# Attention, a Fourier mix and an MLP on one core: a second fold of the Fourier sums, narrower matmuls, layer norm sums by transposes, and a new order

## The chip, the core and the metric

The kernel runs on one core of a Trainium2 chip. A core has TensorE (PE in the profile, with its weight loads shown apart as PEld), VectorE (DVE), ScalarE (ACT), GpSimd (POOL) and SyncE (SP), which here only issues transfers. TensorE multiplies a stationary operand (up to 128 rows by 128 columns, loaded first) with a moving one (128 rows by up to 512 columns) and adds into PSUM, which has eight banks of 512 floats for each of 128 partitions. The metric is the device time of one execution in microseconds (us), the median of the runs.

## The reference, cut to what matters

```python
# q, k, v: (8, 8, 576, 64); s: (8, 8, 576)
scores = q @ k.transpose(0, 1, 3, 2) / 8
cum = np.cumsum(np.maximum(s, 0), -1)
bias = -(cum[..., :, None] - cum[..., None, :])
scores = np.where(causal, -1e9, scores + np.minimum(bias, 0))
attn = np.exp(scores - scores.max(-1, keepdims=True))
x = attn / (attn.sum(-1, keepdims=True) + 1e-9) @ v      # -> (8, 576, 512)
mixed = np.real(np.fft.fft(np.fft.fft(x, axis=1), axis=2))
u = x + mixed
un = (u - mean(u)) / np.sqrt(var(u) + 1e-6)               # over the 512 features
out = u + np.maximum(un @ w_ch1, 0) @ w_ch2               # 512 -> 2048 -> 512
```

## The kernel before

**Attention** runs over 32 pairs of heads (8 batches, 4 pairs each). For a pair `high` and `low` split q and k into two rounded parts, so that one-pass matmuls (float32r) give enough digits; the bias stands as extra rows of the same operands (`KQ`). `maxes` multiplies query chunks of 128 with all keys that they may see (`pm`, line 873) and DVE takes the largest with a causal mask added (`tri`, `trih`; lines 875 and 877). The maxima go by a PE transpose (`pmt`) and a transfer into another row of `KQ`. `scores` multiplies again, the key chunk now stationary (`ps`, lines 930 and 931), ACT writes exp into `P`, POOL clears the triangle. Head 0 is stored reversed and head 1 rotated by 64 positions, so that the corners of 64 keys of both heads share one product (line 941, `Px`). Products with fewer than 256 moving columns are padded to 256. `av` multiplies `va` (V | ones | V, 192 wide, a slice of 128 stationary) with `P` in float32, which takes several passes (`pavA`, `pavB`, lines 966 and 970); one output row is the sum of the weights. `recip` sends the sums through memory (`rd`, `rb`), `finish` scales and lays the result into `xa` and `xs`, in the order of features `_perm`.

**Fourier.** `folds` adds and subtracts features d and 512 - d (`xa` and `xs`) and positions t and 576 - t; `fourier` then multiplies over features with cosine and sine tables (`pzc`, line 677, and `pzs`, line 669: two halves of 128 features by three parts, 256 or 258 columns), over positions (`pyc`, `pys`, lines 691 and 700), and adds the result into `xa` and `xs`, which go to memory as `uD`. Seven batches are mixed in during attention, the eighth at the seam and beside the first MLP pieces.

**MLP.** The 4608 tokens are nine tiles of 512. `ln_tile` loads a tile u, forms mean and variance with a matrix of ones on PE (`spread_sum`, lines 486 and 487; four matmuls of 512 columns a tile) and splits the centred tile into `uch` and `ucl`. `mlp_tile` runs 16 steps f: twelve matmuls into `h` (line 557), ACT `zh`, DVE `zl` (line 562), and twelve matmuls of the step before into `acc` (lines 569 to 571). The end of a tile multiplies by r (line 588), adds u and stores.

**What sets the order.** Streams are written interleaved (`weave`), and `order` then arranges every engine's instructions up to the first whole MLP tile by a list schedule: estimated costs (`cost`), `HOLD`, `SLACK` and a table of rank offsets (`SHIFT`, `SEED`). Each engine works through its queue in that order. PSUM tiles come from two rings, `bank` (3 slots) and `m` (5 slots, attention only), taken in turn.

Of the kernel before, what the change touches and what calls it, by code (L numbers as in the profile page):

```python
# [60 lines left out]
SHIFT = {
    (PE, "acc"): (0, 0, 0, 0, 0, 0, 5866), (PE, "h"): (0, 0, 0, 0, 0, 0, -296), (PE, "mu"): (0, 2583, 0, 0, 0, 0, 341),
    (PE, "p"): (0, 0, 0, 0, -168, 0, -9), (PE, "pavA"): (-335, 0, -14, -4, 0, 52, 0), (PE, "pavB"): (6022, 42, 43, 43, 46, 5789, 0),
    (PE, "pm"): (18, 0, 0, 0, -1, 0, 0), (PE, "pmt"): (193, -48, 3, -2167, -254, 0, 0), (PE, "ps"): (-1361, 2, 0, 0, 3, 0, 0),
    (PE, "pyc"): (0, 0, 0, 54, 58, -602, -3), (PE, "pys"): (0, 0, 0, 6, 2, -61, 1), (PE, "pzc"): (0, 0, 0, -3, 0, -23, -315),
    (PE, "pzs"): (0, 0, -801, -2493, 0, 6667, 418), (PE, "var"): (0, 0, 0, 0, 0, 170, 5872),
    (DVE, "Aw"): (-240, 0, 0, 0, -2067, -16, 0), (DVE, "De"): (0, 0, 0, 0, -4837, 1161, 0), (DVE, "Df"): (0, -935, 0, 0, -12, 653, 0),
    (DVE, "Do"): (0, -201, 0, 0, -30, 0, 0), (DVE, "KQ"): (-267, 0, 0, 0, 0, 0, 0), (DVE, "M"): (-191, -2461, -792, -1216, -5948, 0, 0),
    (DVE, "Px"): (-45, 0, 0, 0, 0, 0, 0), (DVE, "cw"): (-16, 0, 0, 0, 0, 0, 0), (DVE, "e"): (0, 161, 0, 0, 0, 589, 0),
    (DVE, "eh"): (0, 209, 0, 0, 0, 0, 0), (DVE, "eps"): (-18, 0, 0, 0, 0, 0, 0), (DVE, "k"): (0, 95, 63, 117, 135, 0, 0),  # L70
    (DVE, "ones"): (303, 0, 0, 0, 0, 0, 0), (DVE, "part"): (0, 0, 0, 0, 0, 0, -298), (DVE, "r"): (0, 0, 0, 0, 0, -322, 839),
    (DVE, "rows"): (0, 0, 0, 0, -2506, 0, 65), (DVE, "sums"): (0, 52, -54, -2195, -1068, -3432, 0), (DVE, "t"): (0, -81, 0, 0, 0, 181, 8917),
    (DVE, "tl"): (0, -356, 0, 0, 0, 2, 32), (DVE, "trash"): (-131, -10028, -9581, -9808, -6968, 0, 0), (DVE, "u"): (0, 81, 0, 0, 0, 0, 33),
    (DVE, "ucl"): (0, 110, 0, 0, 0, 0, 3631), (DVE, "wbias"): (-109, 0, 0, 0, 0, 0, 0), (DVE, "we"): (-22, -71, -17, -34, 0, 0, 1348),
    (DVE, "wl"): (0, 0, 0, 0, 0, -73, -15), (DVE, "wm"): (423, -31, 50, 75, 35, 0, 1852), (DVE, "xr"): (0, 0, 0, 0, 0, -643, 0),
    (DVE, "ym"): (0, 0, 0, 0, -21, -149, -74), (DVE, "yp"): (0, 0, 0, 0, -1431, 74, -17), (DVE, "z"): (0, 0, 0, -2349, 0, 0, -42),
    (DVE, "zc"): (0, 0, -8299, -5757, 0, 0, 9), (DVE, "zl"): (0, 0, 0, 0, 0, 0, -1170), (DVE, "zs"): (0, 0, -13, 0, 0, -46, -154),
    (ACT, "De"): (0, 0, 0, 0, -41, 0, 0), (ACT, "Do"): (0, -598, 0, 0, 639, -30, 0), (ACT, "KQ"): (548, 1481, 197, 242, 2, 0, 0),
    (ACT, "P"): (0, 2, -444, 21, -4202, 0, 0), (ACT, "Px"): (-433, -5720, -5478, -101, -7966, 0, 0), (ACT, "cumhl"): (253, 0, 0, 0, 0, 0, 0),
    (ACT, "cw"): (823, 0, 0, 0, 0, 0, 0), (ACT, "eh"): (0, 26, 0, 0, 0, 34, 0), (ACT, "k"): (159, 0, 0, 0, 0, 0, 0),  # L80
    (ACT, "mt"): (-32, 112, -256, -58, 54, 0, 0), (ACT, "mu"): (0, 0, 0, 0, 0, 0, -11), (ACT, "part"): (0, 0, 0, 0, 0, 0, 478),
    (ACT, "q"): (62, 0, 0, 0, 0, 0, 0), (ACT, "r"): (0, 0, 0, 0, 0, 485, 153), (ACT, "stage"): (1691, 19, 357, -375, -951, 48, 0),
    (ACT, "sumrow"): (21, 138, -457, 0, 15, -36, 0), (ACT, "th"): (0, -275, 0, 0, 0, 404, 148), (ACT, "u"): (0, -55, 0, 0, 0, 0, 184),
    (ACT, "uch"): (0, 803, 0, 0, 0, 0, -199), (ACT, "we"): (-483, 2962, -459, 1931, 3, 0, 322), (ACT, "wh"): (0, 0, 0, 0, 0, 562, -21),
    (ACT, "yc"): (0, 0, 0, 136, -131, 570, -23), (ACT, "zc"): (0, 0, 4397, 597, 0, -732, -39), (ACT, "zh"): (0, 0, 0, 0, 0, 0, -162),
    (ACT, "zs"): (0, 0, -5, 920, 0, -191, -81),
    (POOL, "Bw"): (0, 0, 0, 0, -5280, 29, 0), (POOL, "KQ"): (248, 0, 0, 0, 0, 0, 0), (POOL, "P"): (428, -114, -255, 1127, -89, 0, 0),
    (POOL, "Px"): (-43, 419, -22, -276, 0, 0, 0), (POOL, "cor"): (0, 0, 0, 0, 278, 0, 0), (POOL, "dtab"): (0, 0, 0, -536, 0, 0, 0),
    (POOL, "ident"): (-117, 0, 0, 0, 0, 0, 0), (POOL, "k"): (291, 0, 0, 0, 0, 0, 0), (POOL, "o"): (0, 0, 0, 0, 0, 0, 5),
# [1186 lines left out]
```

## Time and profile before

| | us |
|---|---|
| median of three runs | 1307.48 |
| lowest of them | 1306.1 |
| profiled execution, its time | 1305.39 |
| profiled execution, its span | 1303.6 |
| first matmul of the program starts at | 10.47 |
| attention with seven Fourier batches | to about 456 |
| the seam: last pair, first tile's layer norm, start of the eighth Fourier batch | 456 to 489 |
| first MLP pieces, weights, eighth Fourier batch | 489 to 782 |
| MLP alone | 782 to 1303 |

In the rows that follow, a group stands as line, engine, operation, what it writes and reads, shape and count; behind the first bar the busy time and the mean of one in ns, behind the second the engine's idle time before it and what ended it. In the timeline rows the first number is the start in us from the span's start, the second how long the merged row lasts. In the waits the three numbers are the total in us, how often, and the longest.

### The profile page before, as it was taken

Reading aid. Unit: us, or ns where it says so; the run is one execution under the profiler, and the core shown is the slowest. Engines: PE = TensorE matmul, PEld = TensorE weight load, DVE = VectorE, ACT = ScalarE, POOL = GpSimd, SP = SyncE. Lnnn points to the kernel's source line nnn. Section 1 sums busy time; section 2 is a strip of 40 time slices with the busy share of each in tenths; the row PEclk is TensorE's granted clock in tenths of the full one; section 3 lists DMA queues with packets and bytes.
Section 4 is the critical chain, followed back from the end, with each engine's and each line's share of the span. In section 5 each row is a group of like instructions: output and inputs, shape, how many; then the busy total and the mean of one; then the engine's idle time right before and its main releaser. Section 6 shows DMA issues by size and latency. Waiting matters only on the chain. (4 is left out here: it accounts for less than half of the span.)

```text
span 1303.6 us, 17683 instructions
## 1 busy us (share of the span) xinstructions
PE 1248.2 (96%) x6102; PEld 1033.9 (79%) x6102; DVE 734.6 (56%) x1660; ACT 527.7 (40%) x1163; POOL 554.7 (43%) x544
## 2 busy tenths in 40 slices
...
GB/s 167 228 193 194 196 207 188 181 187 199 190 227 181 170 146 139 129 111 137 81 49 113 33 51 47 33 97 26 7 97 33 17 81 33 97 1 1 97 1 33
DMA packets 77151, 143.29 MB, mean 110 GB/s; under 512 B 11739, under 2 KB 35667, under 8 KB 75271
## 3 DMA queue, kind: packets, MB, share of 16 engines
...
## 5 line engine op out<-in xcount | busy, mean ns | idle before, releaser
L562 DVE SCALAR_TENSOR_TENSOR zl<-h,zh 128x512 fp32r<-128x512 f32 x144 | 99.0, 688 | 377.1 <-ACT zh L561 376.6
L561 ACT ACTIVATE zh<-h 128x512 fp32r<-128x512 f32 x144 | 86.1, 598 | 494.4 <-PE h L557 404.1
L569 PE MATMUL acc<-zh,wh 128*128 128x512 f32 x576 | 224.8, 390 | 1.1 <-ACT part L578 1.0
L570 PE MATMUL acc<-zh,wl 128*128 128x512 f32 x576 | 224.3, 389 | 0.0
L571 PE MATMUL acc<-zl,wh 128*128 128x512 f32 x576 | 223.8, 390 | 0.1
L557 PE MATMUL h<-uch,wh 128*128 128x512 f32 x576 | 158.3, 396 | 7.6 <-DVE yp L706 5.6
L966 PE MATMUL pavB<-P,va 128*128 128x320 f32 (+1 forms) x512 | 161.6, 410 | 0.0
L557 PE MATMUL h<-uch,wl 128*128 128x512 f32 x576 | 155.6, 392 | 0.0
L557 PE MATMUL h<-ucl,wh 128*128 128x512 f32 x576 | 155.5, 391 | 0.0
L933 ACT ACTIVATE P<-ps 128x320 f32<-128x320 f32 (+3 forms) x320 | 126.9, 426 | 44.8 <-PE ps L931 38.9
L596 POOL TENSOR_TENSOR o<-o,w 128x512 f32<-128x512 f32 x32 | 42.6, 1331 | 218.7 <-issue 213.0
L557 PEld LDWEIGHTS h<-uch,wh 128*128 128x128 f32 x576 | 106.8, 189 | 34.9 <-DVE zl L562 6.6
L873 PE MATMUL pm<-KQ 128*128 128x256 f32 (+2 forms) x352 | 109.7, 369 | 20.4 <-ACT KQ L832 10.5
L569 PEld LDWEIGHTS acc<-zh,wh 128*128 128x128 f32 x576 | 108.1, 188 | 24.8 <-ACT part L578 1.6
L557 PEld LDWEIGHTS h<-uch,wl 128*128 128x128 f32 x576 | 108.7, 189 | 23.7
L557 PEld LDWEIGHTS h<-ucl,wh 128*128 128x128 f32 x576 | 108.4, 189 | 23.0
L571 PEld LDWEIGHTS acc<-zl,wh 128*128 128x128 f32 x576 | 108.1, 188 | 23.2 <-DVE zl L562 0.5
L570 PEld LDWEIGHTS acc<-zh,wl 128*128 128x128 f32 x576 | 108.1, 188 | 22.6
L930 PE MATMUL ps<-KQ 128*128 128x320 f32 (+2 forms) x320 | 115.4, 367 | 8.1 <-DMA KQ<-mt 3.1
L877 DVE CUSTOM_DVE_ANT_0 trash<-pm,tri 128x192 bf16<-128x192 f32 (+3 forms) x224 | 101.2, 478 | 15.7 <-PE pm L873 14.0
L855 POOL TENSOR_TENSOR q<-qk,q 64x576 fp32r<-64x576 f32 x64 | 95.5, 1506 | 26.9 <-DMA q<-KQ 12.1
L931 PE MATMUL ps<-q,k 128*128 128x320 f32 (+2 forms) x320 | 98.7, 314 | 0.0
(161 smaller groups left out, 2068.6 us busy)
## 6 DMA issues: line engine op xcount, KB each, us to landing
...
```

Of the source, the lines that this page charges most:

```text
L557: nc.tensor.matmul(h[:, :n], a[:, j * 128:(j + 1) * 128], b[:, j, :n], start=i == 0, stop=i == 11)
L562: nc.vector.scalar_tensor_tensor(out=zl[:, :n], in0=h[:, :n], scalar=0.0, in1=zh[:, :n].bitcast(F32), op0=ALU.max, op1=ALU.subtract)
L569: nc.tensor.matmul(acc[j][:, :n], a[:, cs], y[:, :n], start=g == lo, stop=False)
L570: nc.tensor.matmul(acc[j][:, :n], b[:, cs], y[:, :n], start=False, stop=False)
L571: nc.tensor.matmul(acc[j][:, :n], a[:, cs], z[:, :n], start=False, stop=g == hi - 1)
L855: nc.gpsimd.tensor_sub(q1[64:128, h], qk[0:64, h], q1[0:64, h].bitcast(F32))
L873: nc.tensor.matmul(p[:, :w], flat(qy)[:, q:q + 128], keys, start=True, stop=True)
L877: nc.vector.tensor_tensor_reduce(out=next(turn)[:, :n], in0=p[:, :n], in1=mask, scale=1.0, scalar=first, op0=ALU.add, op1=ALU.max, accum_o ...
L930: nc.tensor.matmul(p[:, :n], flat(ky)[:, k0:k0 + 128], flat(qy)[:, q0 + a:q0 + a + n], start=True, stop=False)
L931: nc.tensor.matmul(p[:, :n], flat(k1)[:, k0:k0 + 128], flat(q1)[:, q0 + a:q0 + a + n], start=False, stop=True)
L933: nc.scalar.activation(P[:, POFF[c] + lo:POFF[c] + hi], p[:, lo - a:hi - a], AF.Exp, scale=0.125)
L966: nc.tensor.matmul(p[:, u - lo:v - lo], va[:, c, vs], P[:, o:o + v - u], start=c == 0, stop=c == 1 and tg == "A")
```

## The change

`folds` gains a second fold: the sums over features d and 256 - d and their differences are formed before the tables (`Dg`), so that even and odd frequencies need 128 features each. `pzs` and `pzc` keep their number of matmuls, with 128 or 130 columns. The correction rows go by a transfer into `eh`. The features are laid out accordingly (`_perm`, `slots`, `finish`).

In attention both heads stand forward now, head 0 rotated, and no product is padded: `pm` of 128 and 192 columns, `ps` of 64 and 192, the corner as two products of 64 by 64. The two maxima of the longest query chunk are joined by a DVE operation in place of a start value. `va` is V and a column of ones for each head, 65 wide.

For tiles 2 to 8 `ln_tile` takes mean and variance by `fold_sum` and `spread` in place of `spread_sum`. The reciprocal of r of the other tiles is cut in four. In the last tile the fourth output goes in halves, and two of four last additions go to POOL. PSUM and four kinds of SBUF tiles get their slots from a table (`SLOTS`), which the schedule chose. `cost`, `SLACK`, `SHIFT` and `SEED` are new. The core of the diff:

```diff
+    def fold_sum(t):
+        tt = lnp.tile([128, TOK], F32, tag="t2", name="tt")
+        nc.vector.transpose(out=tt, in_=t)
+        s = lnp.tile([128, 16], F32, tag="s16", name="s16")
+        nc.vector.tensor_reduce(out=s, in_=tt.rearrange("p (b i) -> p b i", i=32), axis=AX.X, op=ALU.add)
+        sd = dram.tile([4, 16, 32], F32, tag="sd", name="sd", bufs=2)
+        for g in range(4):
+            nc.sync.dma_start(out=sd[g].rearrange("b j -> j b"), in_=s[32 * g:32 * g + 32])
+        c = lnp.tile([128, 4, 4], F32, tag="c16", name="c16")
+        nc.sync.dma_start(out=c, in_=sd.rearrange("g b j -> g (b j)").rearrange("g (p x) -> p g x", x=4))
+        yield 2.0
+        m = lnp.tile([128, 4], F32, tag="m4", name="m4")
+        nc.vector.tensor_reduce(out=m, in_=c.rearrange("p g x -> p x g"), axis=AX.X, op=ALU.add)
+        return m
+    def spread(dst, m):
+        md = dram.tile([128, 4], F32, tag="md", name="md", bufs=2)
+        nc.sync.dma_start(out=md, in_=m)
+        nc.sync.dma_start(out=dst, in_=md.rearrange("p x -> (p x)").partition_broadcast(128))
...
+        far = t0 >= 2 * TOK and n == TOK
+        if far:
+            m = yield from fold_sum(t)
+            nc.vector.tensor_scalar_mul(m, m, 1.0 / DM)
+            spread(mu, m)
+            yield 2.0
...
-        nc.vector.reciprocal(r[:, :n], r[:, :n])
+            for x in range(0, n, 128):
+                nc.vector.reciprocal(r[:, x:x + 128], r[:, x:x + 128])
...
+        nc.vector.tensor_add(g, dc[0], dc[1])
+        split(De[0][:, 0], De[1][:, 0], g)
+        nc.gpsimd.tensor_sub(g, dc[0], dc[1])
+        split(De[0][:, 1], De[1][:, 1], g)
...
-            for jj in range(2):
-                for x, y in PASS3:
-                    nc.tensor.matmul(p[:96, 0:256], Do[x][:, jj, 96 * c:96 * c + 96], dsin[y][:, jj], start=i == 0, stop=i == 5)
+            for r in range(2):
+                for i, (x, y) in enumerate(PASS3):
+                    nc.tensor.matmul(p[:96, 128 * r:128 * r + 128], Do[x][:, r, 96 * c:96 * c + 96], dsin[y][r], start=i == 0, stop=i == 2)
...
-            w = max(n, 256)
-            nc.tensor.matmul(p[:, :w], flat(qy)[:, q:q + 128], keys, start=True, stop=True)
+            nc.tensor.matmul(p[:, :n], q, keys, start=True, stop=True)
...
-                parts = [(0, 256), (256, 320)] if c == 0 else [(0, w)] if w > 256 else [((w - 256) * h, 256)]
+                parts = [(0, 320), (320, 256)] if c == 0 else [(0, w)]
+                    for u, v in ((0, HALF), (HALF, n)) if c + h + a == 0 else ((0, n),):
...
-                    nc.tensor.matmul(p[:, u - lo:v - lo], va[:, c, vs], P[:, o:o + v - u], start=c == 0, stop=c == 1 and tg == "A")
+                    nc.tensor.matmul(p[:65, u - lo:n], va[:, c, 65 * h:65 * h + 65], P[:, o:o + lo + n - u], start=c == 0, stop=c == 1 and tg == "A")
...
+        n = used[tag] = used.get(tag, -1) + 1
+        k = int(SLOTS[tag][n]) if n < len(SLOTS[tag]) else n % bufs
+        return pool.tile(shape, dtype, tag=f"{tag}.{k}", name=name, bufs=1)
...
+        t = 2 * n / 2.4 + 3 if label(out.tensor) == "pmt" else 4 * max(n / 2.4, load) + 6 if s.reads[0].dtype == F32 else max(n / 2.4, load) + 14
...
-SLACK = {DVE: 200.0, ACT: 145.0, POOL: 103.0, SP: 159.0}
+SLACK = {PE: 26.0, ACT: 34.0, POOL: 133.0}
```

Three places of the new order. First PE's queue at a Fourier product in attention, before (a row is line, operation, what it writes and reads, and the output's shape; `pzs` are the sine products, `ps` scores, `pavB` products with V):

```order
L966 MATMUL pavB<-P,va 128x192
L669 MATMUL pzs<-dtab_80,Do_1173 96x256
L669 MATMUL pzs<-dtab_81,Do_1173 96x256
L669 MATMUL pzs<-dtab_80,Do_1174 96x256
L930 MATMUL ps<-KQ_118 128x320
```

and after:

```order
L992 MATMUL pm<-KQ_120 128x320
L1081 MATMUL pavB<-P,va 65x320
L794 MATMUL pzs<-dtab_80,Do_4327 96x128
L794 MATMUL pzs<-dtab_81,Do_4327 96x128
L794 MATMUL pzs<-dtab_80,Do_4328 96x128
```

The products stand between the same kinds of neighbours, with half the columns and, for V, 65 rows of output.

Second DVE's queue at the seam, where the first tile's layer norm (`r`) meets the end of a Fourier batch (`ym`, `yp` read the products `pys`), before:

```order
L705 TENSOR_TENSOR ym<-yc,pys 128x290
L432 TENSOR_TENSOR tl<-t,th 128x512
L984 TENSOR_SCALAR sums<-sums 32x36
L985 RECIPROCAL sums<-sums 32x36
L524 RECIPROCAL r<-r 128x512
L476 TENSOR_TENSOR wl_6136<-wl_6136,wh_6135 128x512
L706 TENSOR_TENSOR yp<-yc,pys 128x290
```

and after:

```order
L1099 RECIPROCAL sums<-sums 32x36
L613 RECIPROCAL r<-r 128x128
L827 TENSOR_TENSOR ym<-yc,pys 128x290
L613 RECIPROCAL r<-r 128x128
L828 TENSOR_TENSOR yp<-yc,pys 128x290
L613 RECIPROCAL r<-r 128x128 x2
```

`yp` moved from behind the whole reciprocal and a `wl` to behind two quarters of it; on PE the matmuls of `var` moved from behind all `pys` products to ahead of them.

Third DVE's queue in the MLP of tile 2, where the sums of the tiles ahead are taken (`tt` a transpose, `s` and `m` the partial sums and the mean or variance, `c` what came back from memory, `zl` the MLP's own step). Before, at such a place:

```order
L518 TENSOR_TENSOR t_10184<-u 128x512
L519 TENSOR_TENSOR t<-t,t_10184 128x512
L562 SCALAR_TENSOR_TENSOR zl<-h,zh 128x512
L432 TENSOR_TENSOR tl<-t,th 128x512
L497 TENSOR_TENSOR t_10585<-u 128x512
L498 TENSOR_TENSOR t<-t,t_10585 128x512
L562 SCALAR_TENSOR_TENSOR zl<-h,zh 128x512 x2
L432 TENSOR_TENSOR tl<-t,th 128x512
L524 RECIPROCAL r<-r 128x512
```

The order after:

```order
L545 STREAM_TRANSPOSE tt<-t 128x512
L652 SCALAR_TENSOR_TENSOR zl<-h,zh 128x512
L547 TENSOR_REDUCE s_9141<-tt 128x16
L555 TENSOR_REDUCE m_8914<-c_8854 128x4
L607 RECIPROCAL m_8914<-m_8914 128x4
L555 TENSOR_REDUCE m_9208<-c_9148 128x4
L580 TENSOR_SCALAR m_9208<-m_9208 128x4
L593 TENSOR_TENSOR u<-u,mu 128x512 x2
L652 SCALAR_TENSOR_TENSOR zl<-h,zh 128x512
```

and this the same place one tile later:

```order
L547 TENSOR_REDUCE s_9708<-tt 128x16
L555 TENSOR_REDUCE m_9481<-c_9421 128x4
L607 RECIPROCAL m_9481<-m_9481 128x4
L652 SCALAR_TENSOR_TENSOR zl<-h,zh 128x512
L555 TENSOR_REDUCE m_9775<-c_9715 128x4
L580 TENSOR_SCALAR m_9775<-m_9775 128x4
L652 SCALAR_TENSOR_TENSOR zl<-h,zh 128x512
L593 TENSOR_TENSOR u<-u,mu 128x512 x4
```

Before, `tl` fed the sums on PE. Now two round trips through memory lie between `s_9141` and the subtraction of `mu`, in the first place with no `zl` between, in the second with a `zl` between each two steps.

More of the change, by code (lines that the diff above doesn't have):

```diff
@@ L59 @@
 }
-SLACK = {DVE: 200.0, ACT: 145.0, POOL: 103.0, SP: 159.0}
+SLACK = {PE: 26.0, ACT: 34.0, POOL: 133.0}
 SHIFT = {
[L62 to L89, printed above, removed]
-    (POOL, "q"): (303, 0, 1, -28, 73, 0, 0), (POOL, "stab"): (0, 0, 663, 0, 246, 0, 0), (POOL, "t"): (0, -134, 0, 0, 0, -157, -843),
-    (POOL, "tri"): (-234, 0, 0, 0, 0, 0, 0), (POOL, "trih"): (-133, 0, 0, 0, 0, 0, 0), (POOL, "w"): (0, 0, 0, 0, 0, 0, 26),
-    (POOL, "we"): (-7, 2594, 1222, 3207, 17, 0, 0), (POOL, "wl"): (0, 0, 0, 0, 0, -25, -94), (POOL, "xa"): (0, -2173, 0, 0, -2119, -259, -785),
-    (POOL, "xr"): (0, 0, -63, -44, 0, -255, 0), (POOL, "xs"): (0, 0, 0, 0, -4365, -175, -612),
-    (SP, "KQ"): (1054, 52, 0, 253, 8, 0, 0), (SP, "cumD"): (31, 0, 0, 0, 0, 0, 0), (SP, "cw"): (240, 0, 0, 0, 0, 0, 0),
-    (SP, "k"): (20, -2699, -452, -244, -31, 0, 0), (SP, "out_0_dram"): (0, 0, 0, 0, 0, 0, 269), (SP, "part"): (0, 0, 0, 0, 0, 0, -72),
-    (SP, "q"): (12, 0, 87, 2, 130, 0, 0), (SP, "qk"): (1707, 495, 1444, 1234, 631, 0, 0), (SP, "raw"): (4120, 2298, 0, 769, 0, 0, -502),
-    (SP, "rb"): (0, -4958, -2421, -3157, -424, 1311, 0), (SP, "rd"): (0, -24, -1421, -823, 7, -482, 0), (SP, "rows"): (0, 0, 0, 0, 0, -1626, 0),
-    (SP, "sums"): (-15, -1767, 0, 176, -284, 16, 0), (SP, "u"): (0, 0, 0, 0, 0, 0, -284), (SP, "uD"): (0, 0, 0, 0, -1665, 108, 0),
-    (SP, "uch"): (0, 0, 0, 0, 0, 0, 769), (SP, "ucl"): (0, 0, 0, 0, 0, 0, -12), (SP, "va"): (-44, -4091, 5, -1164, -25, 0, 0),
-    (SP, "wD"): (-626, 614, -323, 972, 0, 0, 0), (SP, "wl"): (0, 0, 0, 0, 0, 62, 617), (SP, "xs"): (0, 0, -834, -1668, 0, 52, 0),
-}
@@ L182, in cost @@
     if s.engine == PE:
-        t = 4 * n / 2.4 + 28 if s.reads[0].dtype == F32 and label(out.tensor) != "pmt" else max(n, 256) / 2.4 + 14
+        load = 0.43 * list(out.ap)[0][1]
+        t = 2 * n / 2.4 + 3 if label(out.tensor) == "pmt" else 4 * max(n / 2.4, load) + 6 if s.reads[0].dtype == F32 else max(n / 2.4, load) + 14
         return t, t + 165
@@ L575, in mlp_tile @@
         for j in range(4):
+            if last and j == 3:
+                o = op.tile([128, TOK], F32, tag="o", name="o", bufs=3)
+                for y, (a, b) in enumerate(ends):
+                    nc.vector.tensor_mul(o[:, a:b], r[:, a:b], acc[j][:, a:b])
+                    nc.vector.tensor_add(w[:, j, a:b], w[:, j, a:b], o[:, a:b])
+                    (nc.scalar, nc.sync)[y].dma_start(out=out[j, :, t0 + a:t0 + b], in_=w[:, j, a:b])
+                continue
             if hi < NF:
```

404 lines of the change are left out of this document (253 added, 151 removed).

## The prediction

> **What bounds the kernel now.** I read the page first, then the busy time by stage, then the matmuls' spacing, then what they wait for.
>
> ```profile
> span 1303.6 us, 17683 instructions
> PE 1248.2 (96%) x6102; PEld 1033.9 (79%) x6102; DVE 734.6 (56%) x1660; ACT 527.7 (40%) x1163; POOL 554.7 (43%) x544
> core 0: us, PE busy (x) PEld busy (x) DVE busy (x) ACT busy (x) POOL busy (x), PEclk, DMA share, GB/s
> 130.00:260.00 130.00, 124.20 (x744) 106.78 (x743) 113.79 (x322) 95.06 (x230) 85.65 (x91) 0.99 0.70 193
> 260.00:390.00 130.00, 125.89 (x755) 107.24 (x755) 115.51 (x323) 94.58 (x227) 94.31 (x96) 1.00 0.72 201
> 456.00:489.00 33.00, 24.86 (x120) 21.00 (x119) 28.35 (x49) 17.05 (x35) 21.10 (x18) 0.84 0.46 146
> 782.00:1303.00 521.00, 515.49 (x2270) 425.75 (x2269) 145.14 (x193) 89.61 (x152) 101.84 (x77) 1.00 0.12 44
> ```
>
> TensorE (PE) is the bound: 99% busy in the last 521 us (the MLP alone) and 95 to 97% in attention (to about 456 us), where VectorE (DVE) is nearly full too, at 88 to 89%. Only at the seam, 456 to 489 us, do both wait. A busy share says little of a matmul's price, since matmuls overlap; the distance between starts does:
>
> ```profile
> 501.75 1.07 PE L557 MATMUL h<-uch,wl 128*128 128x512 f32 x4
> 510.84 0.88 PE L669 MATMUL pzs<-dtab,Do 128*96 128x256 f32 x6
> 511.56 0.40 PE L571 MATMUL acc<-zl,wh 128*128 128x512 f32 x1
> ...
> L931 PEld LDWEIGHTS ps<-q,k 128*128 128x128 f32 x320 | 61.4, 193 | 2.5
> L669 PEld LDWEIGHTS pzs<-dtab,Do 128*96 128x96 f32 x144 | 19.4, 163 | 6.9 <-ACT Do L431 2.7 <-DVE Do L432 1.4 <-ACT P L933 0.5
> L909 PEld LDWEIGHTS pmt<-ident,Mx 128*9 128x9 f32 x31 | 2.8, 89 | 4.0 <-DVE Mx L877 2.5
> ...
> 303.38 0.31 PEld L970 LDWEIGHTS pavB<-Px,va 128*128 128x128 f32 x2
> 303.61 0.30 PEld L966 LDWEIGHTS pavB<-P,va 128*128 128x128 f32 x2
> ```
>
> Six matmuls of 256 columns take 511.56 - 510.84 = 0.72 us, 0.120 each: about 256 columns at 0.42 ns and 10 ns. A weight load grows with its stationary columns: (163 - 89) / (96 - 9) = 0.85 ns for each, so about 108 ns of loading for 128 columns, 80 for 96 and 55 for 65. L970 shows that this is a floor: 64 moving columns only, yet its two loads take 303.61 - 303.38 = 0.23 us, 0.115 each. So I price a matmul at the larger of its own columns and the load of the next weights. Below 256 columns the load is the larger one.
>
> **The change, part by part.** 1. Fourier's second fold. 288 matmuls (pzs, pzc) of 256 or 258 columns become as many of 128 or 130, stationary side 96 or 97 wide. By columns alone they would take 65 ns, by the load about 80 and a few: 85. I take the load, the row of the same stationary width. 288 x (0.120 - 0.085) = 10.0 us less, 8.8 in attention and 1.2 for the eighth batch beside the MLP. It adds four operations of 289 columns for each batch, two on DVE and two on POOL; they are priced under rival C.
>
> 2. Unpadded chunks. In maxes, 96 matmuls fall from 256 to 128 or 192 columns, but their 128-wide loads hold them at 108 ns: -1.5 us in all. In scores, for each of 64 (32 pairs, two matmuls a piece), the first stretch is now 64 + 256 + 256 in place of 256 + 320: 0.108 + 0.117 + 0.117 - 0.117 - 0.146 = +0.079; two pieces of 192 save 0.010 each; the corner costs as before (two of 64 columns with 64-wide loads). 64 x 0.059 = +3.8 us: here the change adds time.
>
> 3. V by 65 columns. Of the 64 narrow products (L970) the first of two passes falls from about 0.111 to 0.056 us, the second mostly waits for the next load as before: 64 x 0.067 = -4.3 us. Products of 128 columns and more are held by their own columns: nothing. The smaller V transfer saves 4.7 MB, hidden.
>
> Attention together: -8.8 - 1.5 + 3.8 - 4.3 = -10.8 us. As PE is 95% busy there I let it all through.
>
> The Trainium skill, TensorE: Matmul & The Clock Gate, section Back-to-back issue gap, gives an isolated matmul N/2.4 + 2.5 ns, 56 ns at 128 columns. By that rule the same counts would give 13 us more gain; the same section says that a stream of load and matmul pairs is slower, and the L970 loads above agree with that part. The result is rival B, whose numbers come from columns in the rows above.
>
> 4. Layer norm of tiles 2 to 8 off PE.
>
> ```profile
> L486 PE MATMUL mu<-th,ones 128*128 128x512 f32 x9 | 3.7, 416 | 2.0 <-ACT r L523 1.1 <-ACT th L431 0.9
> 935.74 0.69 DVE L562 SCALAR_TENSOR_TENSOR zl<-h,zh 128x512 fp32r<-128x512 f32 x1 [4.75 <-ACT zh L561]
> 941.18 0.69 DVE L562 SCALAR_TENSOR_TENSOR zl<-h,zh 128x512 fp32r<-128x512 f32 x1 [4.75 <-ACT zh L561]
> 940.58 0.39 PE L570 MATMUL acc<-zh,wl 128*128 128x512 f32 x1
> 940.80 0.39 PE L571 MATMUL acc<-zl,wh 128*128 128x512 f32 x1
> 476.51 0.32 SPq L987 DMA_DIRECT2D rd<-sums  x1
> 479.61 1.18 SPq L990 DMA_DIRECT2D rb<-rd  x2
> 483.44 1.26 DVE L1005 TENSOR_TENSOR xr<-stage,rb 128x576 f32<-128x576 f32 x1
> ```
>
> 28 matmuls of 512 columns go, each 0.227 (four L557 start 0.91 apart from the next group): -6.3 us. In their place stand two exchanges through memory for a mean: DVE transpose and sum, four writes and a read on SP, a small sum on DVE, then a write and a broadcast. DVE is 28% busy in that stage, which hides the transposes and sums themselves. But it waits in order for both exchanges, and zl, which PE needs, is queued behind; on SP the tile's output stores are, and nothing on the chip waits for those. There is slack: zl is due each 5.44 us, and the zl that ended at 936.43 was first used at 940.80, 4.3 us later. One exchange, write and read back, took at most 483.44 - 476.51 = 6.9 us here, other issues between; no row shows writes of 4 bytes. Ends: 3.1 us (issue to issue) and 6.9 or more; I take 5.5, nearer the upper end, since four issues of about 0.5 us come first. In DVE's new order the tiles from 5 on have a zl between the steps: no loss while an exchange stays below 7.2 us. Tile 4's has none: 1.4 + 5.5 + 0.3 + 5.5 + 1.4 + 0.7 = 14.8 us from one zl's start to the next one's end, against 6.1 + 4.3 = 10.4: +4.4 us once. Net -1.9.
>
> The Trainium skill, DMA: Bandwidth & Descriptors, section Rules for kernel authors, speaks against this step: a non-contiguous last dimension becomes one descriptor for each element, here 512 in each of 56 writes. No run so far shows such a write; what a slow one would cost is rival D.
>
> 5. The seam.
>
> ```profile
> 481.56 2.08 PE L557 MATMUL h<-uch,wh 128*128 128x512 f32 x4 [5.59 <-DVE yp L706]
> 486.51 1.09 PE L557 MATMUL h<-uch,wh 128*128 128x512 f32 x4
> 489.26 0.39 PE L486 MATMUL mu<-th,ones 128*128 128x512 f32 x1
> 476.72 3.35 DVE L524 RECIPROCAL r<-r 128x512 f32<-128x512 f32 x1 [0.24 <-ACT r L523]
> 481.06 0.44 DVE L706 TENSOR_TENSOR yp<-yc,pys 128x290 f32<-128x290 f32 x1
> ```
>
> h waits 5.6 us for a bank that yp frees, and yp stands behind a reciprocal of 3.35 us and a wl. After the wait twelve h matmuls take 486.51 - 481.56 = 4.95 us, the next twelve 2.75: the granted clock was 0.84 in this stage, 2.2 us lost. The change cuts the reciprocal in four (0.84 each), puts yp after the second, drops the wl between, and moves var ahead of the pys products. What is left late is yp itself, behind ym: about 1.3 us. 5.6 + 2.2 - 1.3 = -6.5 us.
>
> 6. Tail and head.
>
> ```profile
> 1297.10 0.39 PE L571 MATMUL acc<-zl,wh 128*128 128x512 f32 x1
> 1299.45 0.69 DVE L590 TENSOR_TENSOR u<-u,o 128x512 f32<-128x512 f32 x1
> 6.04 0.67 ACT L431 CAST cumhl<-cw 64x576 fp32r<-64x576 f32 x1 [1.66 <-DVE cw L756]
> 6.22 0.46 DVE L830 CAST KQ<-qk 64x576 fp32r<-64x576 f32 x1 [0.22 <-DMA qk<-in_qkT_dram]
> ```
>
> DVE ends 2.65 us after the last matmul's modelled end at 1297.49. With two of four additions on POOL and the last product in halves of about 0.4 us an operation, some 1.2 us are left: -1.5. At the head the cast moves to DVE, 0.67 against 0.46, with a hand-over less: -0.5.
>
> 7. Slots and new order.
>
> ```profile
> PE pm L873 <- DVE Mx L877: 8.4, 13, 2.5
> PE ps L930 <- ACT P L933: 1.5, 3, 1.0
> ```
>
> These waits, 9.9 us, end when an older tile's reader frees a PSUM slot. Choosing slots by expected release can take all or nothing of them; with an order that could also be worse the ends are -10 and +6. I take a bit over half, -6.
>
> Sum: -10.8 - 1.2 - 1.9 - 6.5 - 1.5 - 0.5 - 6 = -28.4. The profiled execution took 1305.4 us with what lies around its span; the median shown is 1307.5, the lowest 1306.1, so about 1.4 above it at the middle of the two. 1305.4 - 28.4 + 1.4 = 1278 us.
>
> **The rivals.** B: columns alone price a narrow matmul. Fourier then saves 15.1, maxes 3.3, and scores 3.7 in place of costing 3.8; with a tenth of it lost in attention's waits that is 13 us more: 1265. Against it stand the L970 loads.
>
> C: DVE holds attention.
>
> ```profile
> L877 DVE CUSTOM_DVE_ANT_0 trash<-pm,trih 128x256 bf16<-128x256 f32 x32 | 13.4, 418 | 14.3 <-PE pm L873 13.8
> L432 DVE TENSOR_TENSOR De<-Df,De 128x289 fp32r<-128x289 f32 x16 | 11.0, 686 | 0.0
> L707 POOL TENSOR_TENSOR xa<-xa,ym 128x289 f32<-128x289 f32 x16 | 15.5, 970 | 1.1 <-DVE ym L705 1.0
> ```
>
> The fold adds 16 x 0.69 = 11.0 us on DVE and 16 x 0.97 = 15.5 on POOL; half the trih columns save about 32 x 0.13 = 4.2 on DVE, while the joining of two maxima costs about as much. DVE goes to some 90% of a shorter stage. If that keeps the pace, parts 1 to 3 in attention and 7 give nothing: 1278 + 16.8 = 1295.
>
> D: the exchange is slow. At 10 us each, six tiles lose 2 x 10 - 14.5 = 5.5 us and tile 4 loses 13.4 in place of 4.4: 33 + 9 = 42 us more, 1320. It starts to cost at 7.2 us.
>
> E, on the other side: below 256 moving columns a matmul falls back to four passes.
>
> ```profile
> 459.08 0.70 PE L966 MATMUL pavB<-P,va 128*128 128x320 f32 x2
> 459.62 0.82 PE L966 MATMUL pavA<-P,va 128*128 128x256 f32 x4
> ```
>
> The F32 products with V do: one of 320 columns takes 0.54 us, four times 320 x 0.42 ns. 704 narrow matmuls would then cost 84 us more than before in place of 12 less: 1374. Slower than before begins at (1307.5 - 1278) / 704 = 42 ns above my price each; by over 2% at 79 ns. No row has a single-pass matmul below 256, so nothing in the trace excludes it; the smooth 0.42 ns a column from 512 to 256 speaks against it.
>
> **How the numbers follow.** Forecast 0.55 (1268 to 1288), B 0.12, a better order than I allow 0.06, C 0.15, D 0.06, E 0.06. The range 1261 to 1299 leaves out D, E and part of the better order. 2% is about what can be told from no change, 26 us, so faster means below 1281.3: 0.62 of the forecast, B and the better order, 0.52. Within 2%: the rest of the forecast, C and D, 0.42. Slower: E, 0.06.
>
> **What would show it.** pzs groups of six spanning about 0.51 us (0.39 for B, 1.3 for E); ps of 64 columns 0.108 apart; the 4-byte writes' round trip on DVE, m waiting for c, and L571 waiting for zl near tile 4; h at the seam waiting under 2 us with the clock at 1.00; pm waits on Mx below 5 us in total. If DVE is above 93% busy in attention while PE falls under 93%, it is C. The forecast fails if narrow matmuls keep neither price or if the new order opens a wait of more than 20 us.

## The result, and the profile after

The changed kernel takes 1353.96 us (median of 4 runs, 1352.57 to 1356.25), the kernel before 1306.84 beside it: a ratio of 1.036, 95% interval [1.034, 1.038]. It is slower by 47 us, where 28 us less were forecast. One of the four executions of the kernel before took 2511 us; it counts in that median but not in the ratio. The profiled span of the changed kernel is 1351.3 us, against 1303.6 before.

By stage, from the windows of after (columns as in the prediction: busy time of PE, PEld, DVE, ACT and POOL, then the granted clock, the DMA share and GB/s):

```profile
130.00:260.00 130.00, 124.32 (x778) 97.45 (x777) 106.93 (x337) 96.70 (x227) 87.44 (x86) 0.99 0.65 178
456.00:489.00 33.00, 28.76 (x149) 22.07 (x148) 24.83 (x50) 20.85 (x47) 20.98 (x19) 0.84 0.44 142
620.00:782.00 162.00, 148.62 (x622) 119.46 (x622) 78.72 (x130) 33.53 (x67) 58.19 (x47) 0.96 0.27 72
782.00:1351.00 569.00, 545.86 (x2377) 448.13 (x2375) 141.62 (x221) 81.49 (x144) 116.70 (x89) 0.99 0.16 47
```

The loss is where PE was 98 to 99% busy before. In the last stage PE now idles 23 us, from 620 to 782 it stands for 13 us, and from 489 to 620 for 13 us too (117.7 of 131 busy, 129.0 before). The clock is the other part: one minus the mean granted clock, times the span, is 30 us in this execution (0.978) and 9 us before (0.993). Attention is as busy as before, at 95 to 97% from 130 to 390 us, but does not end sooner. Who waits, from the waits of after (total, times, longest):

```profile
DVE m L555 <- DMA c<-sd: 66.8, 13, 9.4
PE acc L662 <- DVE zl L652: 29.4, 15, 3.6
DVE u L593 <- DMA mu<-md: 25.6, 5, 5.6
PE pm L992 <- ACT KQ L953: 14.7, 2, 12.6
```

One exchange, from the timeline of DVE of after (start, duration, instruction, idle time ahead of it in brackets):

```profile
1042.13 0.69 DVE L547 TENSOR_REDUCE s<-tt 128x16 f32<-128x512 f32 x1 [2.23 <-DMA sd<-s]
1045.15 0.69 DVE L652 SCALAR_TENSOR_TENSOR zl<-h,zh 128x512 fp32r<-128x512 f32 x1 [0.31 <-ACT zh L651]
1054.19 0.18 DVE L555 TENSOR_REDUCE m<-c 128x4 f32<-128x16 f32 x1 [8.34 <-DMA c<-sd]
1054.61 0.69 DVE L652 SCALAR_TENSOR_TENSOR zl<-h,zh 128x512 fp32r<-128x512 f32 x1
```

And PE's timeline of after behind it:

```profile
1055.36 0.80 PE L662 MATMUL acc<-zl,wh 128*128 128x512 f32 x1 [2.81 <-DVE zl L652]
1055.95 0.63 PE L660 MATMUL acc<-zh,wh 128*128 128x512 f32 x1
1056.38 0.63 PE L661 MATMUL acc<-zh,wl 128*128 128x512 f32 x1
```

The sum is ready at 1042.82 and its reader starts at 1054.19: 11.4 us, where 5.5 were taken. The zl behind it in DVE's queue is late, PE stands 2.8 us, and the matmuls behind that start 0.43 us apart (1055.95 to 1056.38) in place of 0.23: half clock. That is rival D's mechanism.

How far each kernel is at four points of the MLP, read from the starts of `h` in the traces (us; the first h, the first h of the 4th, the 50th and the last of 144 steps):

```
                 1st     4th     50th    144th
before           481.6   500.8   771.9   1289.2
after            485.3   512.2   800.3   1337.1
before_far       477.1   496.9   797.5   1335.4
sums_on_pe       487.3   513.0   777.4   1294.3
whole_rows       486.0   511.2   776.7   1288.3
px_rows          475.4   501.5   767.1   1278.7
before_rows      483.6   502.7   776.9   1288.5
```

Executions of one kernel differ by up to 15 us here (12 runs of `px_rows`: 1294.0 to 1308.8), so a few us between two traces say little by themselves; spacings, which repeat within 1 or 2 ns, and ratios over many runs say more.

### The profile page after: what moved, and what is told of

The parts are those of the page before. It is cut to its first block, busy times and chain, and to the rows that moved or that the text cites. A ratio compares the mean times of both kernels' runs of the same rounds, so it can differ in the third digit from the quotient of the medians.

```text
span 1351.3 us, 17970 instructions
## 1 busy us (share of the span) xinstructions
PE 1262.8 (93%) x6205; PEld 1010.3 (75%) x6205; DVE 720.1 (53%) x1720; ACT 513.0 (38%) x1115; POOL 570.0 (42%) x529
## 5 line engine op out<-in xcount | busy, mean ns | idle before, releaser
L662 PE MATMUL acc<-zl,wh 128*128 128x512 f32 x577 | 229.1, 398 | 29.4 <-DVE zl L652 29.4
L661 PE MATMUL acc<-zh,wl 128*128 128x512 f32 x577 | 227.6, 395 | 0.0
L647 PE MATMUL h<-uch,wh 128*128 128x512 f32 x576 | 161.3, 395 | 10.4 <-DVE zl L652 9.5
L647 PE MATMUL h<-ucl,wh 128*128 128x512 f32 x576 | 160.4, 392 | 0.0
L647 PE MATMUL h<-uch,wl 128*128 128x512 f32 x576 | 159.5, 392 | 0.0
L1081 PE MATMUL pavB<-P,va 128*65 128x320 f32 (+1 forms) x512 | 157.8, 416 | 0.5 <-ACT stage L1089 0.4
L1048 PE MATMUL ps<-KQ 128*128 128x320 f32 (+4 forms) x352 | 122.1, 359 | 8.7 <-DMA KQ<-mt 4.0
L996 DVE CUSTOM_DVE_ANT_0 trash<-pm,tri 128x320 bf16<-128x320 f32 (+2 forms) x256 | 117.1, 483 | 18.8 <-PE pm L992 17.2
L992 PE MATMUL pm<-KQ 128*128 128x320 f32 (+4 forms) x352 | 107.7, 368 | 16.0 <-ACT KQ L953 14.7
L1049 PE MATMUL ps<-q,k 128*128 128x256 f32 (+4 forms) x352 | 106.4, 315 | 0.9 <-DVE k L973 0.9
```

Of the source, the lines that this page charges most:

```text
L647: nc.tensor.matmul(h[:, :n], a[:, j * 128:(j + 1) * 128], b[:, j, :n], start=i == 0, stop=i == 11)
L661: nc.tensor.matmul(acc[j][:, u:v], b[:, cs], y[:, u:v], start=False, stop=False)
L662: nc.tensor.matmul(acc[j][:, u:v], a[:, cs], z[:, u:v], start=False, stop=g == hi - 1 and v == n)
L992: nc.tensor.matmul(p[:, :n], q, keys, start=True, stop=True)
L996: nc.vector.tensor_tensor_reduce(out=next(turn)[:, :n], in0=p[:, :n], in1=mask, scale=1.0, scalar=NEG, op0=ALU.add, op1=ALU.max, accum_out ...
L1048: nc.tensor.matmul(p[:, u:v], flat(ky)[:, k0:k0 + 128], flat(qy)[:, m:m + v - u], start=True, stop=False)
```

## The experiments

**1. Which part loses the time.** `sums_on_pe` is the changed kernel with the old sums and their old places:

```diff
-        far = t0 >= 2 * TOK and n == TOK
+        far = False
-            ... [later(ln_tile(*tiles[x + 1], 1), 2), 14] if k == 3 else [later(ln_tile(*tiles[x + 1], 1), 4), 18]
+            ... [later(ln_tile(*tiles[x + 1], 1), 3), 12] if k == 3 else [later(ln_tile(*tiles[x + 1], 1), 8), 20]
```

> The changed kernel with the layer norm sums of all nine tiles on TensorE again, written at the places they have before the change. Theory T (the exchange through memory is slow): the trace after shows 10.7 to 11.3 us from the end of a sum on DVE to the landing of c, where 5.5 was forecast, and its MLP stages from the 49th step on last 553.7 us against 514.9 before. Without exchanges that stage should last 515 us again and the stalls between 620 and 797 us (about 18 us) should go as well: 1295 to 1305 us, with no wait of acc for zl over 5 us in total. Rival S (the new order and slots lose the time, the exchange is only where it shows): the time stays above 1330. In both theories attention should be as late as after: the last score product at 455 to 460 us, 5 to 8 us later than before.

`before_far` is the reverse: the kernel before, with `fold_sum`, `spread` and their use in `ln_tile` put in, at the new places.

> The kernel before with the exchange alone: tiles 2 to 8 take mean and variance by the transposes and the transfers, all else as before. Theory T: the same stalls as after, so 1345 to 1365 us, slower by 40 to 55 us. Rival S: 1300 to 1312 us, no difference that can be told.

Measured: 1310.16 us, ratio to before 1.004 [1.0017, 1.0063]; and 1350.85 us, 1.036 [1.033, 1.039]. Theory T held from both sides: the exchange alone makes the kernel before as slow as the whole change does, and without it the changed kernel is 4 us behind the kernel before. But 4 us behind is above the 1295 to 1305 that theory T gave, and it is not 26 ahead: the other parts, forecast at -26.5 together, brought nothing in sum.

**2. What is slow in the exchange.** `whole_rows` keeps both round trips and drops the 4-byte pieces:

```diff
-        sd = dram.tile([4, 16, 32], F32, tag="sd", name="sd", bufs=2)
-        for g in range(4):
-            nc.sync.dma_start(out=sd[g].rearrange("b j -> j b"), in_=s[32 * g:32 * g + 32])
+        sd = dram.tile([4, 32, 16], F32, tag="sd", name="sd", bufs=2)
+        nc.sync.dma_start(out=sd.rearrange("g j b -> (g j) b"), in_=s)
...
-        nc.sync.dma_start(out=c, in_=sd.rearrange("g b j -> g (b j)").rearrange("g (p x) -> p g x", x=4))
+        nc.sync.dma_start(out=c, in_=sd.rearrange("g j b -> g (j b)").rearrange("g (p x) -> p g x", x=4))
...
+            mu = mu.rearrange("p (j b) -> p b j", b=16)
+            r = r.rearrange("p (j b) -> p b j", b=16)
```

> The changed kernel with as many round trips, but no 4-byte pieces: the sums go to memory as 128 rows of 64 bytes in one write in place of four writes of 512 pieces, and mean and r stay in the order of the transposed blocks, which their readers undo with a strided view. Theory T1 (the pieces are what is slow): from the sum to c about 5 us in place of 11, below the 7.2 us at which a loss starts, so that 30 to 40 us come back: 1310 to 1325 us. Rival T2 (each transfer costs its latency whatever its pieces, and two exchanges in a row do it): 9 us or more stay, and the time stays above 1340.

Measured: 1305.96 us, ratio to before 1.0016 [0.9994, 1.0039]: 48 us less than after, T1, and more than it asked. The same sum and reader as above, from the timeline of DVE of `whole_rows`:

```profile
913.96 0.66 DVE L547 TENSOR_REDUCE s<-tt 128x16 f32<-128x512 f32 x1
916.38 0.69 DVE L659 SCALAR_TENSOR_TENSOR zl<-h,zh 128x512 fp32r<-128x512 f32 x1 [1.12 <-ACT zh L658]
919.55 0.18 DVE L554 TENSOR_REDUCE m<-c 128x4 f32<-128x16 f32 x1 [2.47 <-DMA c<-sd]
```

The page's line on packets, of after:

```profile
DMA packets 118470, 141.71 MB, mean 105 GB/s; under 512 B 51103, under 2 KB 75319, under 8 KB 116587
```

And of `whole_rows`:

```profile
DMA packets 90918, 141.70 MB, mean 109 GB/s; under 512 B 23551, under 2 KB 47767, under 8 KB 89035
```

From 914.62 to 919.55 are 4.9 us in place of 11.4, with the same bytes and 27,552 packets fewer (56 writes of 512 pieces were 28,672). The edit also issues one write in place of four, so the issues are a rival cause. The timeline of SP settles it, first of after:

```profile
1042.85 1.90 SPq L550 DMA_DIRECT2D sd<-s  x4
1051.86 0.38 SPq L552 DMA_DIRECT2D c<-sd  x1
```

Then of `whole_rows`:

```profile
914.65 0.32 SPq L549 DMA_DIRECT2D sd<-s  x1
916.13 0.37 SPq L551 DMA_DIRECT2D c<-sd  x1
```

The issues themselves take 1.9 us in place of 0.3. From the last write's issue to the read, which SP holds back until the writes have landed, pass 7.1 us in place of 1.2. So the pieces make up most of the difference and the number of issues 1.6 us of it. Over the nine exchanges of each trace from 800 us on, the sum reaches its reader in 10.4 to 11.4 us in after, and in 3.8 to 6.9 us in `whole_rows` (4.6 to 4.9 where DVE waited for `c`). The Trainium skill, DMA: Bandwidth & Descriptors, section Rules for kernel authors, says that a strided last dimension becomes one descriptor for each element; the packets agree.

`before_rows`, the mended exchange in the kernel before, asks what the step is worth by itself.

> The kernel before with one part of the change alone, mended: the layer norm sums of tiles 2 to 8 by transposes and transfers, with rows of 64 bytes as in whole_rows. Its attention and seam are the kernel before's. Step 4 gave 6.3 us for the 28 products, with nothing lost while an exchange stays under 7.2 us; whole_rows gained 5.9 us on sums_on_pe from the first whole MLP tile to the last (+5.1 against before became -0.9 within the tiles). If that is the price of the step by itself, 1299 to 1303 us, and a tile takes about 1 us less than before. Rival (the exchange loses elsewhere what it gains on TensorE): within 2 us of the kernel before.

Measured: 1305.78 us, ratio 0.999 [0.997, 1.001]: the rival's time. Within the tiles the gain is there: from the 50th step to the last, 511.6 us (776.9 to 1288.5) against 517.3 before, 5.7 us less. Part of it is lost again at the end: from the last step to the end of the span are 16.1 us against 14.5. The whole rows have a price there that the expectation left out, since their readers now step through r with a stride. From the groups of DVE of before:

```profile
L588 DVE TENSOR_TENSOR o<-r,acc 128x512 f32<-128x512 f32 x28 | 19.0, 685 | 25.3 <-PE acc L571 14.1 <-DMA out_dram<-o 11.2
```

And of `before_rows`:

```profile
L631 DVE TENSOR_TENSOR o<-r,acc 128x512 f32<-128x512 f32 x28 | 28.2, 1050 | 24.2 <-PE acc L614 14.2 <-DMA out_dram<-o 10.1
```

The trace of `before_rows` is also 5.0 us late ahead of the 50th step, 2 of them already at the first h. Up to there the two kernels run in the same order but for two places on ACT, so these 2 us are probably scatter; whether the other 3 are the exchange's or scatter, one trace can't tell.

**3. Slots.** `slots_in_turn` is `sums_on_pe` with the table emptied (`SLOTS = {}`).

> As sums_on_pe, but without the table of slots: each tile takes the next slot of its ring in turn, as before the change. My step 7 gave slots and order together 6 us. If the table helps by that much, this is 3 to 8 us slower than sums_on_pe, with the waits of products for a slot's last reader about 5 us longer. If the table itself is why attention gained nothing, it is 5 us or more faster.

Measured: 1316.13 us, ratio 1.0105 [1.007, 1.014] against 1.004. Every engine runs the same order as in `sums_on_pe`, so the table alone is worth 6 us by the medians and some 8 (0.65%) by the ratios, of four runs. In its trace the waits of products for a slot's last reader add up to 11 us against 6, as expected.

**4. The corner product with V.** The spacings in the trace of `sums_on_pe` point at one more place. Before, the product of the corner weights (`Px`) with V went over 128 rows; the changed kernel gives it 64 (`va[:HALF, 4, ...]`), which the prediction had not priced. `px_rows` gives it 128 again:

```diff
-    Ps = [att.tile([HALF, 2, HALF], F32, name=f"Px{i}") for i in range(2)]
+    Ps = [att.tile([128, 2, HALF], F32, name=f"Px{i}") for i in range(2)]
+    for t in Ps:
+        nc.gpsimd.memset(t[HALF:128], 0.0)
...
-  nc.tensor.matmul(p[:65, n - HALF:n], va[:HALF, 4, 65 * h:65 * h + 65], st["Px"][:, h], ...)
+  nc.tensor.matmul(p[:65, n - HALF:n], va[:, 4, 65 * h:65 * h + 65], st["Px"][:, h], ...)
```

> whole_rows with the same order on every engine, but the corner product with V over 128 rows again as before the change: the lower half of Px is zero and is set once, the stationary side is all 128 rows of V's last block, still 65 columns wide. In the trace of sums_on_pe a matmul in front of this product holds PE 0.28 us (300.394 to 300.679, 53 ns of columns), and its weight loads wait 12.3 us in 48 places for nothing that the profile names. Theory H (a product of 64 rows cannot have its weights loaded while one of 128 rows runs, so PE empties ahead of it and behind it): about 0.15 us for each of 64 products comes back, 1294 to 1300 us against 1306. Rival (the rows do not matter, the 65 columns or the neighbours do): within 3 us of whole_rows.

`v_wide` keeps the 64 rows and widens the other side:

```diff
-  nc.tensor.matmul(p[:65, u - lo:n], va[:, c, 65 * h:65 * h + 65], ...)
+  nc.tensor.matmul(p[:, u - lo:n], va[:, c, 2 * h:2 * h + 128], ...)
-  nc.tensor.matmul(p[:65, n - HALF:n], va[:HALF, 4, 65 * h:65 * h + 65], ...)
+  nc.tensor.matmul(p[:, n - HALF:n], va[:HALF, 4, 2 * h:2 * h + 128], ...)
```

> whole_rows with the stationary side of V 128 columns wide again, the corner product still over 64 rows, same order; the second head's rows land in the wrong place, so that its output is not the mix's. My step 3 gave the 65 columns 4.3 us, all in the narrow products. Theory H (rows, not columns, set what the narrow product costs, and its floor of about 0.11 us a record is not the load): within 2 us of whole_rows, with these records still about 0.11 us apart. If the columns count: 4 us slower.

Measured: `px_rows` 1301.34 us, ratio 0.9974 [0.9951, 0.9997], 0.4% below `whole_rows` and just above theory H's range; `v_wide` 1312.62, 1.0053 [1.0029, 1.0078], 0.4% above it. Both keep the order of `whole_rows` on PE (the planner's cost of V's products was held, and the two memsets left out of the plan). The same place in three timelines of PE: two records of 192 columns, the two records of the corner product, and the next score product. After:

```profile
110.28 0.49 PE L1081 MATMUL pavB<-P,va 128*65 128x192 f32 x2
110.69 0.33 PE L1084 MATMUL pavB<-Px,va 64*65 64x64 f32 x2
110.95 0.47 PE L1048 MATMUL ps<-KQ 128*128 128x448 f32 x1
```

`px_rows`:

```profile
107.27 0.49 PE L1090 MATMUL pavB<-P,va 128*65 128x192 f32 x2
107.59 0.28 PE L1093 MATMUL pavB<-Px,va 128*65 128x64 f32 x2
107.68 0.45 PE L1057 MATMUL ps<-KQ 128*128 128x448 f32 x1
```

`v_wide`:

```profile
111.33 0.48 PE L1088 MATMUL pavB<-P,va 128*128 128x192 f32 x2
111.75 0.43 PE L1091 MATMUL pavB<-Px,va 64*128 64x64 f32 x2
112.11 0.47 PE L1055 MATMUL ps<-KQ 128*128 128x448 f32 x1
```

Start to start the three take 0.67, 0.41 and 0.78 us. With 128 rows the corner records cost 0.09 together; with 64 rows 0.26, and the records ahead 0.41 in place of 0.32. Record by record, the median spacings with 64 rows are 0.108 and 0.149 us at 65 columns and 0.160 and 0.202 at 128: 0.052 more each, about what the load of 63 more columns takes (63 x 0.85 ns = 0.054). With 128 rows the first is 0.056, the columns alone. So in these products a load for 64 rows is not hidden behind the running matmul, it is added to it. Theory H held on the rows and fell on the columns: they do count where the load is not hidden.

Before, the same stretch takes 0.46 (0.32 for the 192 columns and 0.14 for the product, 92.53 to 92.67):

```profile
92.53 0.33 PE L970 MATMUL pavB<-Px,va 128*128 128x64 f32 x2
92.67 0.45 PE L873 MATMUL pm<-KQ 128*128 128x448 f32 x1
```

64 such places give 64 x (0.67 - 0.46) = +13.4 us by spacing. Step 3's -4.3 is there once the rows are kept: 64 x (0.41 - 0.46) = -3.2. Spacing is not yet time, though. PE runs the same order in `whole_rows` and `px_rows`, so the places can be paired: 58 pairs at full clock save 0.24 us each on average, 15 us for 64, while the time fell by 0.4%, some 5 us with 4 of uncertainty. About 2 us of the rest went to the clock (experiment 5 has the means); where the others went stays open. For `v_wide` the pairs give +7.0 us, which its +0.4% allows.

**5. The Fourier products.** `fourier_wide` is `whole_rows` with them at their old widths, `px_fourier` is `px_rows` with the same edit; the additional operations of the fold on DVE and POOL stay in both:

```diff
-  nc.tensor.matmul(p[:96, 128 * r:128 * r + 128], Do[x][:, r, 96 * c:96 * c + 96], dsin[y][r], ...)
+  nc.tensor.matmul(p[:96, 0:256], Do[x][:, r, 96 * c:96 * c + 96], dtab[y][:, 258:514], ...)
-  nc.tensor.matmul(p[:n, 130 * r:(130, 258)[r]], De[x][:, r, t0:t0 + n], dcos[y][r], ...)
+  nc.tensor.matmul(p[:n, 0:258], De[x][:, r, t0:t0 + n], dtab[y][:, 0:258], ...)
```

> whole_rows with the Fourier products of 256 and 258 columns again, in the same order and number; it adds both halves of the frequencies into the same columns, so the mix that it computes is another one. My step 1 gave the narrower products 10.0 us, rival B 15. If step 1 holds, this takes 1314 to 1318 us; by B 1319 or more. If attention is held by another engine than PE (rival C), or the narrow products push PE's clock down, it is within 3 us of whole_rows, or faster.

> px_rows with the Fourier products of 256 and 258 columns again, same order; the mix that it computes is another one. On whole_rows the same edit made attention end 4.2 us later (468.8 to 473.0), where step 1 gave 8.8, and the half-clock windows in attention fell from four to one. If that repeats, so if about half of the fold's gain is lost to the clock because narrower products keep PE less busy, attention ends 3 to 6 us later than in px_rows (460.1) and its half-clock windows fall from five to three or fewer. If the fold's gain arrives in full: 8 us or more later.

Measured: `fourier_wide` 1311.54 us, 1.0058 [1.0034, 1.0081], 0.4% above `whole_rows`; `px_fourier` 1301.47, 0.996 [0.993, 0.999], 0.1% below `px_rows`. Taken together the old widths cost about 2 us with some 3 of uncertainty, not 10; the two results lie 7 us apart, slightly more than their intervals explain. In the trace of `px_fourier` attention ends at 464.3, 4 us later, as expected; its half-clock windows fell only from five to four, and its median shows no loss. The products themselves have the price of step 1; here six of 130 columns take 0.48 us (timeline of PE of after), 0.08 each:

```profile
520.04 0.65 PE L800 MATMUL pzc<-dtab,De 128*96 128x130 f32 x6
520.52 0.31 PE L801 MATMUL pzc<-cor,eh 97*96 97x258 f32 x1
```

Part of the gain goes back to the clock. The mean granted clock over all runs is 0.9874 for `whole_rows` (10 runs) and 0.9902 with the wide products (5); 0.9857 for `px_rows` (12) and 0.9901 with them (10). One minus the clock, times the span, is an estimate of the time lost to it: 16.5 and 12.9 us, 18.7 and 12.9. So by this estimate 4 to 6 of the 10 us return as half clock; the rest is within the uncertainty or went into waits. How a half-clock stretch arises, from windows of after:

```profile
112.90:116.40 3.50, 3.50 (x22) 2.43 (x21) 3.47 (x4) 1.72 (x6) 3.50 (x4) 1.00 0.99 340
116.40:119.80 3.40, 1.32 (x11) 1.00 (x10) 2.50 (x4) 3.22 (x5) 1.36 (x2) 1.00 0.95 232
119.80:126.60 6.80, 6.59 (x17) 4.16 (x18) 5.75 (x20) 5.88 (x12) 3.25 (x5) 0.50 0.99 260
```

PE is busy for 1.3 of 3.4 us, and the next 6.8 us run at 0.50. The Trainium skill, TensorE: Matmul & The Clock Gate, section What's actually happening, has a free-running window of 3413 ns whose activity sets the next clock; the stretches here agree: in the clock records of after every half-clock stretch but the last lasts 3.41 or 6.83 us. Counting columns at 0.42 ns in that trace, the windows that a half-clock one follows hold 0 to 0.39 of their length in columns, but three others with 0.38 or 0.39 kept the full clock, so the counts give no sharp limit. That narrower products bring more windows under it is argued from these counts; shown is that width alone moves the clock.

**6. The seam.** The wait of h went as forecast (5.6 to 0.6 us), but the stage is no shorter. The timeline of PE of after:

```profile
485.35 1.18 PE L647 MATMUL h<-uch,wh 128*128 128x512 f32 x4 [0.58 <-DVE yp L828]
498.73 1.22 PE L662 MATMUL acc<-zl,wh 128*128 128x512 f32 x2 [3.60 <-DVE zl L652]
512.24 0.62 PE L647 MATMUL h<-uch,wh 128*128 128x512 f32 x2
```

DVE's of after, at the same time:

```profile
495.38 0.76 DVE L745 TENSOR_TENSOR Aw<-xa,xs 128x576 f32<-128x576 f32 x1 [1.96 <-DMA xs<-xr]
496.17 1.54 DVE L747 TENSOR_TENSOR Df<-Aw 128x289 f32<-128x289 f32 x1
497.63 0.45 DVE L764 TENSOR_TENSOR Ds<-Bw 128x288 f32<-128x288 f32 x1
498.00 0.68 DVE L652 SCALAR_TENSOR_TENSOR zl<-h,zh 128x512 fp32r<-128x512 f32 x1
```

PE's of before, the first h of the fourth step:

```profile
500.85 0.39 PE L557 MATMUL h<-uch,wh 128*128 128x512 f32 x1
```

From the first h to the fourth step are 26.9 us, against 19.3 before (481.56 to 500.85). zl stands behind `Aw`, which waits for a transfer. `zl_ahead` holds Aw back in the planner until both zl are placed (an entry for Aw in `HOLD`), `px_zl` does it in `px_rows`, and `seam_by_hand` moves instructions of `px_rows` after the plan.

> whole_rows with one edit of the order: the first sum of the last batch's folds (Aw) may not stand ahead of the first two zl on DVE. In the traces of after and of sums_on_pe zh is there at 493.0, but zl stands behind Aw, which waits 1.8 us for the transfer of xr; acc waits 3.5 us for zl, and PE then runs two windows at half clock. Theory: 4 to 8 us come back, 1298 to 1302. Rival (what is won at this place is lost at the next, since weights and folds are then later): within 2 us of whole_rows.

> px_rows and zl_ahead together. If both theories hold and the gains add: 1288 to 1296 us, which would be the first version faster than the kernel before. If either gives nothing, 1296 or more.

> px_rows with three instructions moved after the schedule, nothing planned anew: the first two zl stand ahead of the last batch's Aw on DVE, and the twelve h of the third step stand ahead of the first sine product on PE. In the trace of px_rows acc waits 3.6 and 1.7 us for these zl and PE then runs at half clock, while the sine product could not start before 495.9 (ACT's Do) in any order. Theory (zl behind Aw was the wait that took the place of the removed one, and only as much is won as PE has other work for until the folds are ready): the h of the third step, 2.75 us, are out of the way by then and the second batch of weights finds PE free: 2 to 5 us less than px_rows. Rival (the folds decide, nothing ahead of them matters): within 1 us of px_rows in the traces, from the first h to the first sine product.

Measured: `zl_ahead` 1318.2 us, 1.0099 [1.007, 1.013], 11 us slower than `whole_rows`; `px_zl` 1308.75, 1.0027 [1.000, 1.005], 7 us slower than `px_rows`; `seam_by_hand` 1301.92, 0.9964 [0.994, 0.9988], the same as `px_rows`. What is late next, from the timeline of PE of `zl_ahead`:

```profile
517.45 0.42 PE L802 MATMUL pzs<-dtab,Do 128*96 128x128 f32 x1 [13.21 <-ACT Do L484]
```

And of `seam_by_hand`:

```profile
483.96 1.18 PE L664 MATMUL h<-uch,wh 128*128 128x512 f32 x4 [0.58 <-DVE yp L845]
505.89 0.39 PE L811 MATMUL pzs<-dtab,Do 128*96 128x128 f32 x2 [3.25 <-ACT Do L493]
510.03 1.20 PE L664 MATMUL h<-uch,wh 128*128 128x512 f32 x2
```

With zl ahead, PE runs out of work sooner and stands at the sine product, which waits for the folds; in `seam_by_hand` the fourth step comes 26.1 us after the first h, as without the moves. My theory fell and the rival held: the folds decide here. From the first Aw to the first sine product are 12.0 us in after (495.38 to 507.37) and 11.7 in `seam_by_hand` (494.16 to 505.89), against 6.8 before (487.94 to 494.73). The second fold's first product needs both halves of the features, the fold before only one; that this is what lengthens it is read from the code and the two timelines, and was not tried by itself. `zl_ahead` is slower than even the rival allowed: holding Aw back made everything behind it late. And the longer stretch is not all lost: from the fourth step to the 50th `sums_on_pe` takes 264.4 us and `whole_rows` 265.5, against 271.1 before, so that from the first h to the 50th step they need 290.1 and 290.7 us, and the kernel before 290.3.

## Why the prediction was wrong, step by step

**What bounds the kernel** was right: PE is the bound wherever time was lost, and rivals C and E did not happen (DVE is 82% busy from 130 to 260 us; narrow products keep their price).

**Step 4 failed, and decided the sign.** It took 5.5 us for an exchange. That is close to what the round trip takes in whole rows (4.9), but the 4-byte writes make it 10.4 to 11.4. The chain of the step was right: DVE waits in order, zl behind it, loss above 7.2 us. -1.9 became +44.7, measured alone. The row that it was taken from (`rd` to `rb`) has no strided side, so it could not show this; the prediction itself named the 512 descriptors of each write, and gave rival D 0.06 all the same. D's place and mechanism were right, and its price of 42 us was close (44.7 + 1.9 = 46.6 measured); its 1320 was short because the rest of the forecast's gain was under it.

**Step 3 had the right price for the wrong product.** 65 columns do save 3.2 us by spacing at 128 rows; the same line of the diff takes 64 rows, and costs 13.4 by spacing, of which the runs gave back about 5 when the rows were restored. This line was in the prediction's own diff and its rows were not read.

**Step 1**: the products cost what was said (0.08 against 0.085 us). Letting the whole gain through because PE is 95% busy was the failure: an estimated 4 to 6 of 10 us went to the clock, and the time moved by about 2.

**Step 2** was not tested by itself, but the trace of `whole_rows` speaks against its largest term. For the first stretch of the scores it priced the records of 64 columns by their loads, at 0.108 us. The two such records of a stretch hold PE for 0.133 and 0.112 (medians of 31 places at full clock), near that price, but the record of 256 columns behind them holds PE for 0.203 where 0.118 is usual, which the step did not foresee: about 32 x 0.085 = 2.7 us more than the +3.8. Its -1.5 for the maxes is also -1.2 by its own prices, 96 x (0.120 - 0.108).

**Step 5** was right that h would wait under 1.3 us, and wrong that nothing else was late: the stage stays at a clock of 0.84, and the stretch to the fourth step is 7.6 us longer in after (5.9 to 6.4 in `whole_rows` and `sums_on_pe`, which win it back by the 50th step). The next late one, the folds, was in the change itself (its first sine product now waits for both halves), and step 1 had priced them only as load on DVE and POOL.

**Step 6**: the head is later, not earlier. The first matmul starts at 12.63 instead of 10.47, waiting for ACT's KQ. The tail gave little: from the last matmul's start to the end of the span are 6.14 us in after and 6.54 before, 0.4 less where 1.5 were forecast. In that trace one of the last half additions on DVE (L671, 256 columns) takes 1.11 us while one of POOL's runs, and the next 0.41 with POOL idle, so the additions moved to POOL seem to slow those left on DVE; that was not tried by itself.

**Step 7**: the table of slots is worth 6 to 8 us, where the forecast took 6 for slots and order together and 10 at most; pm waits on Mx are almost gone, as the prediction asked. What the rest of the new order is worth was not separated.

The best versions found are `px_rows` and `seam_by_hand`: the whole change with whole rows in the exchange and 128 rows in the corner product, 0.3 and 0.4% below the kernel before, with intervals that just exclude no change.
